# Order of work around stage changes in a fused attention and mixture-of-experts kernel

## The chip, the cores and the metric

The kernel runs on one core of one Trainium2 chip. The metric is the device time of one execution in microseconds (us); the median of three runs before the change is 936.39 us (933.29 to 939.31).

The engines of the core are TensorE (PE, matmuls; PEld, its weight loads), VectorE (DVE), ScalarE (ACT), GpSimd (POOL) and SyncE (SP). Each runs its own list of instructions in order. SP issues nearly all transfers here. SBUF is the memory of the engines, PSUM that of matmul results.

## The reference

Three parts follow each other; N is 1792 tokens of 768 numbers.

```
attn   = sigmoid(q @ k^T / 8 - log(448));  x = attn @ v          # 4 batches, 12 heads, 448 x 64
logits = x @ w_gate; each token is assigned to one of 8 experts, 224 tokens to each, greedily by logit
x[e]   = relu(x[e] @ w1[e]) @ w2[e]                              # 768 -> 1024 -> 768, every expert
h      = relu(x @ w_in); g = s * h * h + b                       # 768 -> 2048
out    = g @ w_out                                               # 2048 -> 768
```

All of it is float32. The kernel gets near that precision by splitting each operand into a high and a low half of a shorter format and summing three products: high·high, high·low, low·high.

## The kernel before, in words

**Stages.** Attention and routing come first and are not touched. Then come two passes, `Q` = 0 and 1, of two groups each (group `g` = 2Q + h). A group takes two experts (224 tokens each; 8 units of `w1`, 6 units of `w2`), then the *middle layer* on their 448 tokens: 16 units `f` of `w_in`, 18 matmuls of 448 columns each. After two groups comes the *output stage* of the pass: seven products (index `j`) of four units each, on 3 blocks of 128 tokens (Q = 0) or 4 (Q = 1), 6 matmuls of 384 columns per unit and block. The seven products are a Strassen-like scheme of a 2 x 2 block multiplication; sums of weight blocks for it (T1 to T4) are made on the chip.

**A unit of weights.** SP loads it into `raw` (4 buffers), ACT writes the high half `wh` (L204), DVE or POOL the low half `wl` (L215). `advance()` keeps these ahead of use: loads by 8 units, low halves by 4, high halves by 5.

**What stands around the stage changes.**

- `x_split(e, n)`: four calls transpose the gathered rows of expert `e` on PE (L667) and split them (ACT L669, DVE L670). For the first expert of the next group the calls come in the middle layer; for the second, in the first expert's units 1 to 4. The tiles are named `x` and have two buffers.
- The *late work* (`late_step`, L761 to L785) runs in the two middle layers of Q = 0 only. It turns the last eight blocks of `w_out`, which come as 64-bit numbers, into float32 (`to_float`, three steps; L152, L153, then L155, then L157) and makes the sums (L776 and L780 to L782), for four indices `u`: two per middle layer, one step per unit. Loads go into `orow`, sums into another buffer of the name `x`; the results are stored to DRAM, from where the output stage loads them as weights.
- `a_high` (ACT L827) and `a_low` (DVE L833) split the middle layer's result `gt` for the output stage, `a_sum` (DVE L818 to L822) adds parts of it. The first two pieces are split at the end of the middle layer, into `u`; the rest in the output stage, into the buffers `as`.
- The *results* of a product: after its fourth unit each block is copied (ACT L889) or added (DVE L892) from PSUM to the rows `orow`. Product 2 starts on the PSUM banks of product 1, product 6 on those of product 5.

The order on each engine is that of the program text; no planner stands behind it.

Of the kernel before, what the change touches and what calls it, by code (L numbers as in the profile page):

```python
# [30 lines left out]
KG = F2 // 128  # L31
HT = (128, CAP - 128)
DH = DM // 2
# [30 lines left out]
def tile_kernel(ctx, tc, qT, kT, v, wg, w1, w2, wi, wo, s2, b2, cst, out):  # L64
    nc = tc.nc
    V, A, G, T = nc.vector, nc.scalar, nc.gpsimd, nc.tensor
# [634 lines left out]
    def advance():  # L701
        while nu["dma"] < min(nu["use"] + 8, len(units)):
            w_dma()
        while nu["low"] < min(nu["use"] + 4, nu["high"]):
            w_low()
        while nu["high"] < min(nu["use"] + 5, len(units)):
            w_high()

    def expert(e, y):
        x = xg.pop(e)  # L710
        u = ml.tile([128, KF, 2, CAP], F32R, name="u")
        for f in range(KF):
            wh, wl = w_get()
            if f < KF - 2:
                half_mm(wh, wl, x, KD, AF.Relu, (u[:, f, 0], u[:, f, 1]), f < KF - 3)
                if f == KF - 3:
                    advance()
            else:
                short_mm(wh, wl, x, KD, (u[:, f, 0], u[:, f, 1]))
                if f == KF - 2:  # L720
                    advance()
            if 1 <= f <= 4:
                if e % 2 == 0:
                    x_split(e + 1, f - 1)
                if out_rows:
                    scatter(*out_rows.pop(0))
        sl = slice((e % 2) * CAP, (e % 2 + 1) * CAP)
        for d in range(KD):
            wh, wl = w_get()
            half_mm(wh, wl, u, KF, AF.Copy, (y[:, d, 0, sl], y[:, d, 1, sl]), d < KD - 1)  # L730
            if not e and d == 1:
                row_ids()

    def scatter(ids, row):
        G.memset(spacer, 0.0)
# [16 lines left out]
    def flat(t):  # L752
        return t.rearrange("p k c -> p (k c)")

    def late_step(u, k):
        o, x = late["o"], late["x"]
# [3 lines left out]
        s, c, d = (x[:, 768 * n:768 * n + 768] for n in range(3))  # L760
        first, second = LB + u, LB + 4 + u  # L761
        if k in (0, 4):
            to_float(a if k == 0 else b, r, raw, 0)
        elif k in (1, 5):
            to_float(a if k == 1 else b, r, raw, 1)
            nxt = second if k == 1 else first + 1
            if nxt < LB + 4 or k == 1:
                late_in(nxt)
        elif k == 2:
            to_float(a, r, raw, 2)  # L770
        elif k == 3:
            nc.sync.dma_start(c, flat(blocks[0][0][u]))
            nc.sync.dma_start(d, flat(blocks[1][0][u]))
        elif k == 6:
            to_float(b, r, raw, 2)
            V.tensor_sub(s, fa, fb)  # L776
            nc.sync.dma_start(flat(narrow[second]), fb)
            nc.sync.dma_start(flat(T3[u]), s)
        elif k == 7:
            V.tensor_sub(fa, fa, c)  # L780
            V.tensor_sub(c, c, s)
            V.tensor_sub(d, d, c)  # L782
            nc.sync.dma_start(flat(T1[u]), fa)
            nc.sync.dma_start(flat(T2[u]), c)
            nc.sync.dma_start(flat(T4[u]), d)  # L785

    stores, out_rows, late, pool = [], [], {}, {}
    na = {"sum": 0, "high": 0, "low": 0}
# [44 lines left out]
        V.tensor_sub(a[:, 1], part(st, i, operand[i // 4]), a[:, 0].bitcast(F32))  # L833
        na["low"] += 1

    def a_advance(st, n):
        while na["low"] < min(n + 3, na["high"]):
            a_low(st)
        while na["sum"] < min(n + 5, 28):
            a_sum(st)  # L840
        while na["high"] < min(n + 4, 28):
            a_high(st)

    def outputs(st):
# [19 lines left out]
        a_advance(st, 0)  # L864
        for j in range(7):
            spans = [[u] for u in range(4)] if j < 6 or not Q else [[0], [1], [2, 3]]
            for span in spans:
                ws = {u: [w.rearrange("p k c -> p (k c)") for w in w_get()] for u in span}
                for p in range(P):
                    acc = bank[j][p][:, :DH]  # L870
                    for u, c in ((u, c) for u in span for c in range(2)):
                        wh, wl = ws[u]
                        a = st["slots"][(4 * j + u) % st["ring"]]
                        cols = slice(c * DH, (c + 1) * DH)
                        hi, lo = (a[:, n, c, p * 128:(p + 1) * 128] for n in range(2))
                        T.matmul(acc, hi, wh[:, cols], start=(opens[j] and u == 0 and c == 0), stop=False,  # L876
                                 skip_group_check=True)
                        T.matmul(acc, hi, wl[:, cols], start=False, stop=False, skip_group_check=True)  # L878
                        T.matmul(acc, lo, wh[:, cols], start=False, stop=(u == 3 and c == 1), skip_group_check=True)  # L879
                advance()  # L880
                a_advance(st, 4 * j + span[-1] + 1)
                if span[-1] < 3:
                    continue
                for p in range(P):
                    acc = bank[j][p][:, :DH]
                    c11, c12 = (row[2 * p][:, d * DH:(d + 1) * DH] for d in range(2))
                    c21, c22 = (row[2 * p + 1][:, d * DH:(d + 1) * DH] for d in range(2))
                    if j in (0, 2, 3, 6):
                        A.copy({0: c11, 2: c22, 3: c21, 6: c12}[j], acc)  # L889
                    else:  # L890
                        dst = {1: c11, 4: c21, 5: c22}[j]
                        V.tensor_add(dst, acc, dst)  # L892
                    if j in (5, 6):
                        h = 6 - j
                        out_rows.append((tok[p][h], row[2 * p + h]))
                        if Q:
                            scatter(*out_rows.pop(0))

    for n in (0, 2, 1, 3):
        x_split(0, n)  # L900
# [5 lines left out]
    for Q in range(2):  # L906
        epool = ExitStack()
        pool["y"] = epool.enter_context(tc.tile_pool(name=f"yp{Q}", bufs=1))
        for h in range(2):
# [8 lines left out]
            for f in range(KG):  # L918
                wh, wl = w_get()
                p = ps_m.tile([128, 512], F32, name="acc")  # L920
                for k in range(KD):
                    full_mm(p[:, :S], wh[:, k], wl[:, k], y, k, k == 0, k == KD - 1)
                r = pool["y"].tile([128, S], F32, name="tmp", bufs=2)
                A.activation(r, p[:, :S], AF.Relu)  # L924
                V.scalar_tensor_tensor(r, r, sb2[:, 0:1], r, op0=ALU.mult, op1=ALU.mult)  # L925
                if h and f < KG // 2:
                    V.scalar_tensor_tensor(gn[:, f, 1], r, sb2[:, 1:2], gn[:, f, 0], op0=ALU.add, op1=ALU.subtract)
                else:
                    A.activation(gn[:, f, h], r, AF.Identity, bias=sb2[:, 1:2])
# [12 lines left out]
            gather(2 * g + 3)  # L942
        epool.close()
# [66 lines left out]
```

## Time and profile before

| | |
|---|---|
| median of 3 runs | 936.39 us |
| profiled execution | 934.25 us, of which the traced span is 932.4 us |
| PE busy | 890.1 us, 95% of the span |
| DVE busy | 625.1 us, 67% |
| ACT busy | 516.8 us, 55% |
| POOL busy | 137.3 us, 15% |
| data moved | 177.80 MB, mean 191 GB/s |

In the span, the first group begins at about 204 us, its middle layer at 272.8, the second group at 332 and its middle layer at 399.8. The first output stage starts at 459.9 us, the third group at 558, the fourth at 681, and the second output stage runs from 803.8 us to the end.

"Busy" is an average over all of that; where an engine stood idle, and what ended it, is in the list of waits. A time given in a trace row is the start, in us from the beginning of the span; the number behind it is the duration.

### The profile page before, as it was taken

Reading aid. Unit: us, or ns where it says so; the run is one execution under the profiler, and the core shown is the slowest. Engines: PE = TensorE matmul, PEld = TensorE weight load, DVE = VectorE, ACT = ScalarE, POOL = GpSimd, SP = SyncE. Lnnn points to the kernel's source line nnn. Section 1 sums busy time; section 2 is a strip of 40 time slices with the busy share of each in tenths; the row PEclk is TensorE's granted clock in tenths of the full one; section 3 lists DMA queues with packets and bytes.
Section 4 is the critical chain, followed back from the end, with each engine's and each line's share of the span. In section 5 each row is a group of like instructions: output and inputs, shape, how many; then the busy total and the mean of one; then the engine's idle time right before and its main releaser. Section 6 shows DMA issues by size and latency. Waiting matters only on the chain.

```text
span 932.4 us, 14229 instructions
## 1 busy us (share of the span) xinstructions
PE 890.1 (95%) x5291; PEld 769.1 (82%) x5291; DVE 625.1 (67%) x1005; ACT 516.8 (55%) x871; POOL 137.3 (15%) x131
## 2 busy tenths in 40 slices
PE   9999999789999979999799999999999999899997
PEld 4555545569889979999699999999989999899997
DVE  3777886638566787869767857864467764547680
ACT  6667667726555556643645546655565634554540
POOL 1000003213510034200000015410034100000003
PEclk9999999769999999999999999999999999999999
DMA  9989893855656776648643347753365633332313
GB/s 296 323 295 349 298 328 138 247 154 186 199 170 223 259 278 211 226 156 282 220 148 119 120 136 238 273 161 120 102 193 181 218 116 104 102 100 87 100 34 135
DMA packets 70184, 177.80 MB, mean 191 GB/s; under 512 B 8160, under 2 KB 25056, under 8 KB 70112
## 3 DMA queue, kind: packets, MB, share of 16 engines
q1 hardware_dynamic: 67840, 165.85, 54.4%
q0 software_dynamic: 2272, 11.01, 3.3%
q8 instruction: 42, 0.69, 0.3%
q14 instruction: 30, 0.25, 0.1%
HBM read 148.52 MB, written 28.31 MB: 190 GB/s over the span
## 4 chain that ended last, share of the span: by engine, by line
PE 56%; issue 23%; DVE 8%; DMA 5%; ACT 4%; POOL 3%; POOLq 0%; SPq 0%; ACTq 0%; DVEq 0%
PE pv L274 8%; PE psc L263 7%; PE acc L743 6%; PE acc L745 6%; PE acc L744 6%; PE acc L675 6%; DMA raw<-in_w_dram 4%; PE acc L879 3%; PE acc L876 3%; DVE wl L215 3%; PE acc L878 3%; PE acc L676 3%; ACT wh L204 2%; DVE y L689 1%; POOL wl L215 1%
## 5 line engine op out<-in xcount | busy, mean ns | idle before, releaser
L204 ACT CAST wh<-raw 128x768 fp32r<-128x768 f32 (+1 forms) x232 | 202.4, 879 | 115.7 <-issue 46.8
L215 DVE TENSOR_TENSOR wl<-raw,wh 128x768 fp32r<-128x768 f32 (+1 forms) x191 | 200.5, 1052 | 54.5 <-ACT wh L204 54.4
L215 POOL TENSOR_TENSOR wl<-raw,wh 128x768 fp32r<-128x768 f32 (+1 forms) x41 | 91.3, 2234 | 490.1 <-ACT wh L204 485.6
L743 PE MATMUL acc<-y,wh 128*128 128x448 f32 x384 | 141.2, 368 | 0.0
L744 PE MATMUL acc<-y,wh 128*128 128x448 f32 x384 | 140.4, 366 | 0.0
L745 PE MATMUL acc<-y,wl 128*128 128x448 f32 x384 | 140.3, 365 | 0.0
L675 PE MATMUL acc<-u,wh 128*128 128x448 f32 x384 | 121.7, 376 | 3.0 <-DVE u L699 2.9
L925 DVE SCALAR_TENSOR_TENSOR tmp<-tmp,sb 128x448 f32<-128x448 f32 x64 | 45.6, 712 | 83.5 <-ACT tmp L924 83.3
L676 PE MATMUL acc<-u,wl 128*128 128x224 f32 x384 | 101.4, 264 | 0.0
L675 PE MATMUL acc<-x,wh 128*128 128x448 f32 x288 | 95.0, 384 | 3.8 <-DVE x L670 3.4
L265 ACT ACTIVATE attn<-psc,nls 112x896 f32<-112x896 f32 x96 | 88.9, 1009 | 10.1 <-PE psc L263 10.1
L675 PEld LDWEIGHTS acc<-u,wh 128*128 128x128 f32 x384 | 72.1, 188 | 9.9 <-DVE u L699 4.6
L924 ACT ACTIVATE tmp<-acc 128x448 f32<-128x448 f32 x64 | 34.9, 546 | 80.1 <-PE acc L745 80.1
L274 PE MATMUL pv<-attn,vt 112*64 112x448 f32 x384 | 77.5, 545 | 0.0
L676 PE MATMUL acc<-x,wl 128*128 128x224 f32 x288 | 76.8, 267 | 0.5 <-DVE wl L215 0.5
L745 PEld LDWEIGHTS acc<-y,wl 128*128 128x128 f32 x384 | 72.1, 188 | 5.9
L743 PEld LDWEIGHTS acc<-y,wh 128*128 128x128 f32 x384 | 72.1, 188 | 5.8
L744 PEld LDWEIGHTS acc<-y,wh 128*128 128x128 f32 x384 | 72.2, 188 | 5.7
L676 PEld LDWEIGHTS acc<-u,wl 128*128 128x128 f32 x384 | 73.3, 191 | 0.0
L675 PEld LDWEIGHTS acc<-x,wh 128*128 128x128 f32 x288 | 54.9, 191 | 8.4 <-DVE x L670 3.9
L274 PEld LDWEIGHTS pv<-attn,vt 112*64 112x64 f32 x384 | 25.4, 136 | 42.9 <-issue 36.1
L680 DVE TENSOR_TENSOR tmp<-acc,tmp 128x224 f32<-128x224 f32 x96 | 36.9, 385 | 32.0 <-ACT tmp L679 32.0
(261 smaller groups left out, 1744.2 us busy)
## 6 DMA issues: line engine op xcount, KB each, us to landing
raw<-nw SPq DMA_DIRECT2D x88, 384.0 KB, 3.1
raw<-in_w_dram SPq DMA_DIRECT2D x64, 384.0 KB, 3.0
raw<-in_w_dram SPq DMA_DIRECT2D x48, 512.0 KB, 5.0
craw<-in_wi_dram SPq DMA_DIRECT2D x16, 768.0 KB, 4.5
raw<-mx SPq DMA_DIRECT2D x32, 384.0 KB, 2.8
nw<-co SPq DMA_DIRECT2D x24, 384.0 KB, 8.2
craw<-in_wo_dram SPq DMA_DIRECT2D x8, 768.0 KB, 4.2
orow<-in_wo_dram SPq DMA_DIRECT2D x8, 768.0 KB, 5.7
```

What stands on the lines that cost most here:

```text
L204: A.copy(h[:, :k], raws[i][:, :k])
L215: eng.tensor_sub(lo[:, :k], r[:, :k], h[:, :k].bitcast(F32))
L263: T.matmul(p[:, j, :S], kx[me, 1, c * CP:(c + 1) * CP], qx[me, 0], start=(m == 0), stop=(m == len(terms) - 1))
L265: A.activation(attn[n][:, :, c, :], p[:, :, :S], AF.Sigmoid, bias=nls[:CP], scale=1.0 / math.sqrt(D))
L274: T.matmul(pv[j * 64:(j + 1) * 64, :S], v[:, c, j * D:(j + 1) * D], a[:, j, c, :], start=(c == 0), stop=(c == NC - 1))
L675: T.matmul(p[:, :2 * CAP], wh[:, k], src[:, k].rearrange("p a s -> p (a s)"), start=(k == 0), stop=False)
L676: T.matmul(p[:, :CAP], wl[:, k], src[:, k, 0], start=False, stop=(k == n - 1))
L680: V.tensor_add(tt, p[:, :CAP], bs)
L743: T.matmul(p, wh, src[:, k, 0], start=first, stop=False)
L744: T.matmul(p, wh, src[:, k, 1], start=False, stop=False)
L745: T.matmul(p, wl, src[:, k, 0], start=False, stop=last)
L925: V.scalar_tensor_tensor(r, r, sb2[:, 0:1], r, op0=ALU.mult, op1=ALU.mult)
```

## The change

It moves work and adds or removes no computation.

- The next group's rows are split at units 3, 6, 9 and 12 of the middle layer, not 3, 7, 11 and 15.
- The late work follows a written plan: index `a` = 2h in units 0 to 4, `b` = 2h + 1 in units 4 to 12. The conversion for index 0 is begun in the second layer of expert 1 (`d` = 2, 3, 4), that for index 2 in units 13 and 14 of the first middle layer.
- The first two splits of `gt` are made at units 11 to 14 (`a_high` at 11 and 13, `a_low` at 12 and 14). Before, these were at 14 and 15, with the second `a_low` at the start of the output stage.
- At the end of a product the results are issued in turn with the low halves of weights, the low halves of `gt` and the sums; the high halves follow. Before, the results came behind all of these.

```diff
@@ -730,6 +739,8 @@
             if not e and d == 1:
                 row_ids()
+            if e == 1 and 2 <= d <= 4:
+                late_do(f"a{d - 2}", 0)
@@ -752,37 +763,46 @@
-    def late_step(u, k):
+    def late_do(what, u):
...
-        if k in (0, 4):
-            to_float(a if k == 0 else b, r, raw, 0)
-        elif k in (1, 5):
-            to_float(a if k == 1 else b, r, raw, 1)
...
+    def late_work(h, f):
+        a, b, c = 2 * h, 2 * h + 1, 2 * h + 2
+        plan = {0: [("a2", a) if h else None, ("b0", a), ("load", a)], 1: [("b1", a), ("b2", a)], 2: [("t3", a)],
+                3: [("t1", a), ("t2", a)], 4: [("t4", a), ("a0", b)], 5: [("a1", b), ("a2", b)], 7: [("load", b)],
+                8: [("b0", b)], 9: [("b1", b), ("b2", b)], 10: [("t3", b)], 11: [("t1", b), ("t2", b)],
+                12: [("t4", b)], 13: [None if h else ("a0", c)], 14: [None if h else ("a1", c)]}
...
-    def a_advance(st, n):
-        while na["low"] < min(n + 3, na["high"]):
-            a_low(st)
-        while na["sum"] < min(n + 5, 28):
-            a_sum(st)
+    def ahead(st, n, more=()):
...
+        w_dmas()
+        work, more = [w_lows, lows, sums], list(more)
+        while work or more:
+            for q in (work, more):
+                if q:
+                    q.pop(0)()
+        w_highs()
         while na["high"] < min(n + 4, 28):
             a_high(st)
@@ -877,24 +908,26 @@
-                advance()
-                a_advance(st, 4 * j + span[-1] + 1)
+                n = 4 * j + span[-1] + 1
                 if span[-1] < 3:
+                    ahead(st, n)
                     continue
...
+                ahead(st, n, [lambda p=p: result(p) for p in range(P)])
@@ -927,17 +960,17 @@
-                if f % 4 == 3:
-                    x_split(2 * g + 2, f // 4)
+                if f % 3 == 0 and 3 <= f <= 12:
+                    x_split(2 * g + 2, f // 3 - 1)
                 advance()
                 if not Q:
-                    late_step(2 * h + f // 8, f % 8)
-                if h and f == KG - 3:
+                    late_work(h, f)
+                if h and f == KG - 6:
                     st = start_out(Q)
                     st["ring"] = 6 - Q
-                if h and f >= KG - 2:
+                if h and f in (KG - 5, KG - 3):
                     a_high(st)
-                if h and f == KG - 1:
+                elif h and f in (KG - 4, KG - 2):
                     a_low(st)
```

In the plan `a0` to `a2` and `b0` to `b2` are the three conversion steps of the two blocks of an index; `load` fetches the two other blocks, `t3`, `t1`, `t2`, `t4` make and store the sums.

Three places in the order of the instructions follow. First VectorE at the change from the second middle layer (units 14 and 15) to the first output stage; L925 and L958 are the squares of a unit, L833 and L853 `a_low`, L776 to L782 and L785 to L794 the late sums. Before:

```order
L776 TENSOR_TENSOR x<-orow 128x768
L925 SCALAR_TENSOR_TENSOR tmp<-tmp,sb_76 128x448
L670 TENSOR_TENSOR x<-px,x 128x3x96
L215 TENSOR_TENSOR wl<-raw,wh 128x768
L780 TENSOR_TENSOR orow<-orow,x 128x768
L781 TENSOR_TENSOR x<-x 128x768
L782 TENSOR_TENSOR x<-x 128x768
L833 TENSOR_TENSOR u<-gt,u 128x768 x2
```

and in the changed kernel, from unit 12 on:

```order
L670 TENSOR_TENSOR x<-px,x 128x3x96
L215 TENSOR_TENSOR wl<-raw,wh 128x768
L794 TENSOR_TENSOR x<-x 128x768
L853 TENSOR_TENSOR u<-gt,u 128x768
L958 SCALAR_TENSOR_TENSOR tmp<-tmp,sb_76 128x448
L215 TENSOR_TENSOR wl<-raw,wh 128x768
L958 SCALAR_TENSOR_TENSOR tmp<-tmp,sb_76 128x448
L215 TENSOR_TENSOR wl<-raw,wh 128x768
L853 TENSOR_TENSOR u<-gt,u 128x768
L958 SCALAR_TENSOR_TENSOR tmp<-tmp,sb_76 128x448
L215 TENSOR_TENSOR wl<-raw,wh 128x768 x2
L853 TENSOR_TENSOR as_5376<-gt,as_5376 128x768
```

The row split, the late sums and both `a_low` now stand ahead of unit 15's square (the last L958 shown); behind it come weights, then the third `a_low`.

Second, VectorE at the change from the first group to the second, before (L680 is the first work of expert 2):

```order
L925 SCALAR_TENSOR_TENSOR tmp<-tmp,sb_76 128x448
L670 TENSOR_TENSOR x<-px,x 128x3x96
L215 TENSOR_TENSOR wl<-raw,wh 128x768
L780 TENSOR_TENSOR orow<-orow,x 128x768
L781 TENSOR_TENSOR x<-x 128x768
L782 TENSOR_TENSOR x<-x 128x768
L680 TENSOR_TENSOR tmp<-acc,tmp 128x224
```

and now, from unit 12 on:

```order
L670 TENSOR_TENSOR x<-px,x 128x3x96
L794 TENSOR_TENSOR x<-x 128x768
L958 SCALAR_TENSOR_TENSOR tmp<-tmp,sb_76 128x448
L215 TENSOR_TENSOR wl<-raw,wh 128x768
L152 TENSOR_SCALAR orow<-orow 128x768
L153 TENSOR_SCALAR orow<-orow 128x768
L958 SCALAR_TENSOR_TENSOR tmp<-tmp,sb_76 128x448
L155 SCALAR_TENSOR_TENSOR orow<-orow 128x768
L958 SCALAR_TENSOR_TENSOR tmp<-tmp,sb_76 128x448
L215 TENSOR_TENSOR wl<-raw,wh 128x768
L680 TENSOR_TENSOR tmp<-acc,tmp 128x224
```

Between unit 15's square and expert 2 there is now one low half of weights; the row split and the three sums have gone ahead.

Third, VectorE at the end of product 1 of the first output stage (L892 and L924 are results, L818 and L838 sums), before:

```order
L215 TENSOR_TENSOR wl<-raw,wh 128x768
L833 TENSOR_TENSOR as_5376<-gt,as_5376 128x768
L215 TENSOR_TENSOR wl<-raw,wh 128x768
L833 TENSOR_TENSOR as_5377<-gt,as_5377 128x768
L818 TENSOR_TENSOR gt<-gt 128x2x384
L892 TENSOR_TENSOR orow<-acc,orow 128x384 x3
L215 TENSOR_TENSOR wl<-raw,wh 128x768
```

and now:

```order
L853 TENSOR_TENSOR as_5377<-gt,as_5377 128x768
L215 TENSOR_TENSOR wl<-raw,wh 128x768
L924 TENSOR_TENSOR orow<-acc,orow 128x384
L853 TENSOR_TENSOR as_5378<-gt,as_5378 128x768
L924 TENSOR_TENSOR orow<-acc,orow 128x384
L838 TENSOR_TENSOR gt<-gt 128x2x384
L924 TENSOR_TENSOR orow<-acc,orow 128x384
L215 TENSOR_TENSOR wl<-raw,wh 128x768
```

The first result stands behind one low half of weights, where it stood behind that, a split and a sum.

## Rows read from the trace of the kernel before

**Rows 1.** The page, part 1: busy us (share of the span) xinstructions.
```profile
PE 890.1 (95%) x5291; PEld 769.1 (82%) x5291; DVE 625.1 (67%) x1005; ACT 516.8 (55%) x871; POOL 137.3 (15%) x131
```

**Rows 2.** Waits of PE: waiter <- who ended it: us in total, times, longest.
```profile
PE acc L879 <- DVE u L833: 9.5, 2, 6.9
...
PE px L667 <- DVE x L670: 3.9, 2, 3.1
PE acc L675 <- DVE x L670: 3.4, 2, 1.7
...
PE acc L876 <- DVE orow L892: 2.0, 3, 1.1
```

**Rows 3.** Timeline of PE, first output stage's start: start, duration, instruction [idle before].
```profile
467.30 0.69 PE L879 MATMUL acc<-wh,u 128*128 128x384 f32 x1 [6.85 <-DVE u L833]
...
470.35 0.41 PE L879 MATMUL acc<-wh,u 128*128 128x384 f32 x1
470.60 0.34 PE L876 MATMUL acc<-wh,u 128*128 128x384 f32 x1
```

**Rows 4.** Timeline of PE, second output stage's start.
```profile
808.41 0.51 PE L876 MATMUL acc<-wh,u 128*128 128x384 f32 x1
...
811.60 0.44 PE L878 MATMUL acc<-wl,u 128*128 128x384 f32 x1
```

**Rows 5.** Timeline of DVE, end of the second middle layer.
```profile
460.50 0.68 DVE L925 SCALAR_TENSOR_TENSOR tmp<-tmp,sb 128x448 f32<-128x448 f32 x1 [0.24 <-ACT tmp L924]
...
463.44 0.95 DVE L780 TENSOR_TENSOR orow<-orow,x 128x768 f32<-128x768 f32 x1
...
466.30 1.82 DVE L833 TENSOR_TENSOR u<-gt,u 128x768 fp32r<-128x768 f32 x2
```

**Rows 6.** Chain that ended last, change to the second group: start, us, what.
```profile
335.95 2.54 DVE orow L780
...
340.49 3.93 DMA mx<-x
...
345.08 0.57 DVE x L670
```

**Rows 7.** Timeline of DVE, end of product 1, first output stage.
```profile
488.31 0.96 DVE L215 TENSOR_TENSOR wl<-raw,wh 128x768 fp32r<-128x768 f32 x1 [1.29 <-ACT wh L204]
...
491.43 0.96 DVE L215 TENSOR_TENSOR wl<-raw,wh 128x768 fp32r<-128x768 f32 x1 [1.29 <-ACT wh L204]
...
493.17 0.95 DVE L818 TENSOR_TENSOR gt<-gt 128x768 f32<-128x768 f32 x1
494.04 1.48 DVE L892 TENSOR_TENSOR orow<-acc,orow 128x384 f32<-128x384 f32 x3
```

**Rows 8.** Timeline of PE, second layers of experts 5 and 7.
```profile
608.14 0.47 PE L675 MATMUL acc<-u,wh 128*128 128x448 f32 x1 [0.80 <-DVE u L699]
...
732.18 0.47 PE L675 MATMUL acc<-u,wh 128*128 128x448 f32 x1 [0.35 <-DVE u L699]
```

**Rows 9.** Groups of DVE instructions, 272 to 460 us: busy us, mean ns.
```profile
L155 DVE SCALAR_TENSOR_TENSOR orow<-orow 128x768 int32<-128x768 int32 x8 | 7.6, 952 | 0.0
...
L152 DVE TENSOR_SCALAR orow<-orow 128x768 int32<-128x768 int32 x8 | 4.4, 553 | 0.0
```

**Rows 10.** Timeline of DVE, last work of expert 1.
```profile
274.24 0.39 DVE L689 TENSOR_TENSOR y<-tmp,y 128x224 fp32r<-128x224 f32 x1 [0.45 <-ACT y L688]
```

**Rows 11.** Timeline of PE, first unit of the first middle layer.
```profile
275.81 0.36 PE L743 MATMUL acc<-y,wh 128*128 128x448 f32 x1
276.01 0.36 PE L744 MATMUL acc<-y,wh 128*128 128x448 f32 x1
```

**Rows 12.** Stretches: us, busy of PE, PEld, DVE, ACT, POOL, PEclk, DMA share, GB/s.
```profile
432.00:446.00 14.00, 14.00 (x71) 12.72 (x70) 11.86 (x17) 6.28 (x10) 0.00 (x0) 1.00 0.89 319
...
396.00:460.00 64.00, 64.00 (x327) 58.81 (x326) 49.25 (x70) 28.76 (x50) 1.28 (x1) 1.00 0.62 211
```

**Rows 13.** Timeline of ACT, first output stage's start.
```profile
463.54 1.56 ACT L827 CAST as<-gt 128x768 fp32r<-128x768 f32 x2
```

More of the change, by code (lines that the diff above doesn't have):

```diff
@@ L699, in short_mm, with w_dmas, w_lows, w_highs @@
         V.scalar_tensor_tensor(lo, p, 0.0, hi.bitcast(F32), op0=ALU.max, op1=ALU.subtract)
-    def advance():
+    def w_dmas():
         while nu["dma"] < min(nu["use"] + 8, len(units)):
             w_dma()
+    def w_lows():
         while nu["low"] < min(nu["use"] + 4, nu["high"]):
             w_low()
+    def w_highs():
         while nu["high"] < min(nu["use"] + 5, len(units)):
             w_high()
+    def advance():
+        w_dmas()
+        w_lows()
+        w_highs()
     def expert(e, y):
@@ L753, in flat @@
         return t.rearrange("p k c -> p (k c)")
-    def late_step(u, k):
-        o, x = late["o"], late["x"]
+    def late_do(what, u):
+        o = late["o"]
         a, b, r = (o[:, 768 * n:768 * n + 768] for n in (3 + u % 2, 5, 2))
@@ L759, in late_step @@
         fa, fb = a.bitcast(F32), b.bitcast(F32)
-        s, c, d = (x[:, 768 * n:768 * n + 768] for n in range(3))
-        first, second = LB + u, LB + 4 + u
-        if k in (0, 4):
-            to_float(a if k == 0 else b, r, raw, 0)
-        elif k in (1, 5):
-            to_float(a if k == 1 else b, r, raw, 1)
-            nxt = second if k == 1 else first + 1
-            if nxt < LB + 4 or k == 1:
-                late_in(nxt)
-        elif k == 2:
-            to_float(a, r, raw, 2)
-        elif k == 3:
+        if what[0] in "ab" and what[1:].isdigit():
+            step = int(what[1:])
+            to_float(a if what[0] == "a" else b, r, raw, step)
+            nxt = LB + 4 + u if what[0] == "a" else LB + u + 1
+            if step == 1 and (what[0] == "a" or u < 3):
+                late_in(nxt)
+            if what == "b2":
+                nc.sync.dma_start(flat(narrow[LB + 4 + u]), fb)
+            return
@@ L772, in late_step @@
+        s, c, d = (late["x"][:, 768 * n:768 * n + 768] for n in range(3))
+        if what == "load":
             nc.sync.dma_start(c, flat(blocks[0][0][u]))
             nc.sync.dma_start(d, flat(blocks[1][0][u]))
-        elif k == 6:
-            to_float(b, r, raw, 2)
+        elif what == "t3":
             V.tensor_sub(s, fa, fb)
-            nc.sync.dma_start(flat(narrow[second]), fb)
             nc.sync.dma_start(flat(T3[u]), s)
-        elif k == 7:
+        elif what == "t1":
             V.tensor_sub(fa, fa, c)
+            nc.sync.dma_start(flat(T1[u]), fa)
+        elif what == "t2":
@@ L781, in late_step @@
             V.tensor_sub(c, c, s)
+            nc.sync.dma_start(flat(T2[u]), c)
+        else:
             V.tensor_sub(d, d, c)
-            nc.sync.dma_start(flat(T1[u]), fa)
-            nc.sync.dma_start(flat(T2[u]), c)
             nc.sync.dma_start(flat(T4[u]), d)
+    def late_work(h, f):
[4 more added lines that the diff above has]
+                12: [("t4", b)], 13: [None if h else ("a0", c)], 14: [None if h else ("a1", c)]}
+        for job in plan.get(f, []):
+            if job:
+                late_do(*job)
@@ L834, in a_low, with lows, sums @@
         na["low"] += 1
-    def a_advance(st, n):
-        while na["low"] < min(n + 3, na["high"]):
-            a_low(st)
-        while na["sum"] < min(n + 5, 28):
-            a_sum(st)
+    def ahead(st, n, more=()):
+        def lows():
+            while na["low"] < min(n + 3, na["high"]):
+                a_low(st)
+        def sums():
+            while na["sum"] < min(n + 5, 28):
+                a_sum(st)
+        w_dmas()
+        work, more = [w_lows, lows, sums], list(more)
[3 more added lines that the diff above has]
+                    q.pop(0)()
+        w_highs()
         while na["high"] < min(n + 4, 28):
@@ L863, in outputs @@
             tok.append([idt[:, t - 1, 2 * Q + h:2 * Q + h + 1] if t else idl[:, h:h + 1] for h in range(2)])
-        a_advance(st, 0)
+        ahead(st, 0)
         for j in range(7):
@@ L879, in outputs, with result @@
                         T.matmul(acc, lo, wh[:, cols], start=False, stop=(u == 3 and c == 1), skip_group_check=True)
-                advance()
-                a_advance(st, 4 * j + span[-1] + 1)
+                n = 4 * j + span[-1] + 1
                 if span[-1] < 3:
+                    ahead(st, n)
                     continue
-                for p in range(P):
+                part_of = {0: (0, 0), 1: (0, 0), 2: (1, 1), 3: (1, 0), 4: (1, 0), 5: (1, 1), 6: (0, 1)}[j]
+                def result(p):
+                    t, d = part_of
+                    dst = row[2 * p + t][:, d * DH:(d + 1) * DH]
                     acc = bank[j][p][:, :DH]
-                    c11, c12 = (row[2 * p][:, d * DH:(d + 1) * DH] for d in range(2))
-                    c21, c22 = (row[2 * p + 1][:, d * DH:(d + 1) * DH] for d in range(2))
                     if j in (0, 2, 3, 6):
-                        A.copy({0: c11, 2: c22, 3: c21, 6: c12}[j], acc)
+                        A.copy(dst, acc)
                     else:
-                        dst = {1: c11, 4: c21, 5: c22}[j]
                         V.tensor_add(dst, acc, dst)
                     if j in (5, 6):
-                        h = 6 - j
-                        out_rows.append((tok[p][h], row[2 * p + h]))
+                        out_rows.append((tok[p][t], row[2 * p + t]))
                         if Q:
                             scatter(*out_rows.pop(0))
+                ahead(st, n, [lambda p=p: result(p) for p in range(P)])
     for n in (0, 2, 1, 3):
```

## The prediction

> **What bounds the kernel now.** I read the page's part 1 first: TensorE is busy for 890.1 of 932.4 us [rows 1], so it sets the time, and only what makes it wait, or slows it, can be won. Next its list of waits [rows 2]. The reader is to see four rows that belong to stage changes: 9.5 us for the low half of a piece of `gt` (L833), in two waits, the longest 6.9; 3.9 for the low half of expert rows inside an expert (3.1 of them one wait); 3.4 in two waits of 1.7 for the same thing at an expert's start; 2.0 in three waits for a result to leave its bank. Then the timeline of TensorE at both output stages' starts [rows 3, 4]: behind each long wait there is a stretch of slow steps. Then VectorE at the same places, for what stood ahead of the thing waited for [rows 5, 7], and the chain of waits at the second group [rows 6].
>
> **The change, part by part.** All sums stand against the profiled execution, 934.25 us, of which 932.4 is the span.
>
> *First splits of `gt`.* At the first output stage TensorE stands 6.85 us until L833 [rows 3]. On VectorE this split comes after unit 15's square (460.50), a row split, a low half and the three late sums (from 463.44), and starts at 466.30 [rows 5]. In the new order it is made in unit 12. Its input was finished in the middle layer before (index 0 of `gt`), so nothing holds it there. The wait goes: 6.85, and at the second output stage the other one of the row, 9.5 - 6.85 = 2.65 [rows 2, 3].
>
> *The clock behind these waits.* From 467.30 to 470.35 nine steps take 3.05 us [rows 3]; at full speed a unit of 18 such matmuls takes 3.12, the distance of two low halves of weights in this stage [rows 7], so 0.173 a step, and nine take 1.56. By its steps (0.34 each) TensorE ran near the lower of its two clock levels, 1.2 of 2.4 GHz, after standing still; that cost 1.49. From 808.41 to 811.60 ten steps take 3.19 against 1.73: 1.46 [rows 4]. Without the waits I take both as gone, 2.95; at worst both stay.
>
> What is late next there: the splits of pieces 2 and 3, made in the output stage as before. ScalarE makes their high halves at 463.54, 0.78 each [rows 13], VectorE the low ones after one low half of weights, so the first is ready near 463.54 + 0.78 + 0.96 + 0.91 = 466.2 (0.91 is half of the 1.82 in [rows 5]). TensorE, unheld, reaches unit 2 two units of 3.12 after the stage's start at about 460, at 466.2, and the low half is that unit's third matmul, 0.35 later. ScalarE has a row split and one high half fewer ahead of these than before, so there is more room than that. I take 0; the other end is a wait that takes the place of part of the old one (a rival).
>
> *Row splits at 3, 6, 9, 12.* The two waits of 1.7 [rows 2] are for the last quarter of the rows, split behind unit 15. It moves to unit 12, three units earlier. A unit is 18 steps of 0.20 [rows 11], 3.6 us, so it is 11 us earlier: 3.4 go. The same instructions lie elsewhere in the middle layer, where VectorE is busy 49.25 of 64 us in the fuller of the first two [rows 12]. Cost 0.
>
> *Late sums done by unit 12.* The wait of 3.1 in expert 2 is for a buffer `x` that still holds the last sum: the sums run from 335.95 (the first takes 2.54 us), the last store is issued at 340.49 and takes 3.93 to land, and only then are the rows of expert 3 split [rows 6]. Now this store is issued three units earlier, before expert 2 begins. The 3.1 go.
>
> *Results between splits.* At the end of product 1 the three results start at 494.04, behind low half, split and sum (491.43 to 494.04), and TensorE waits for the bank of the first one [rows 7]. Now the first result is next behind the low half of 491.43, so at about 492.3, 1.7 us sooner; the wait was 1.1 [rows 2]. The other two follow one split or sum apart (0.9 us), and TensorE needs their banks one block (3.12 / 3 = 1.04 us) apart, so they keep up. The three waits go: 2.0.
>
> *What it costs.* (1) Three conversion steps lie in the second layer of expert 1: at most 2 x 0.55 + 2 x 0.95 = 3.0 us of VectorE [rows 9]. Its last work for the layer now ends at 274.63 [rows 10]; TensorE reads that block's low half at 276.01 [rows 11]. Room 1.4. VectorE also idles ahead of it (0.45 in that row alone), so between 0 and 3.0 - 1.4 = 1.6 is lost; I take 0. (2) In the second middle layer units 0 to 5 are over-full: two elementwise steps of about 0.7 each (one is the 0.68 in [rows 5]), a low half of 0.96 and up to 2.0 of late work is 4.4 at most, against 3.6. VectorE falls back by up to 0.8 a unit, some 3 us, until the empty units 6 and 7. Cover: low halves run four units ahead, 14 us. If that cover were gone, TensorE would wait 3 us once. I take 0. (3) SyncE issues the late loads and stores between weight loads, in one queue. The dense units move, each five, two loads and four to five stores of 384 KB, one load of 768 KB and five weight loads of 384 KB: 5.5 MB in 18.2 us, 302 GB/s. The old order's dense stretch ran at 319 with TensorE busy 14.00 of 14.00 us [rows 12]. Cost 0; the other end is the slower rival.
>
> *What is given back.* An expert pair that starts without a wait finds VectorE and the loads less far ahead. The third group is such a start now, and waits 0.80 in its second half; the fourth, which began with a wait, only 0.35 [rows 8]; the second shows no such row. I let both end at 0.80: 0.45 + 0.80 = 1.25, and count 1.6 for what smaller waits may join. Bounds: 0 and twice that.
>
> **Sum:** 6.85 + 2.65 + 2.95 + 3.4 + 3.1 + 2.0 = 20.95, less 1.6: 19.35. 934.25 - 19.35 = 914.9. The profiled execution lies 2.1 under the median of the runs (936.39); I add a little of that and say **915.5**, its own range 911.5 to 919.
>
> A rule of the Trainium skill speaks against one piece. TensorE: Matmul & The Clock Gate, Architectural detail, says that ScalarE and VectorE take their work strictly first in, first out. The trace agrees: the results at 494.04 wait behind a sum they have nothing to do with [rows 7]. By that rule each result now holds what stands behind it, which is the first rival.
>
> **The rivals.**
>
> *Held splits, 919.* A result waits for its block of the last unit, and high halves, low halves and sums stand behind it in order. On ScalarE the next high half starts one result later, 1.48 / 3 = 0.49 [rows 7], at eight product ends; if it were on the path, 8 x 0.49 = 3.9 would come back: 934.25 - 19.35 + 3.9 = 918.8. For it: ScalarE's high half does gate VectorE's low half (1.29 idle, [rows 7]). Against it: that low half is for a unit three to four ahead, some 9 us. Chance 0.09.
>
> *The entry still waits, 923.* Pieces 2 and 3 or the first weights come late, and half of the entry waits stays, with the slow clock in full: 0.5 x 9.5 + 2.95 = 7.7, giving 922.6. For it: my margin above was small. Against it: it counts ScalarE work that no longer stands ahead. Chance 0.09.
>
> *The waits are not what they seem, 932.* Another thing, ready only just before, stood behind each (weights, a transfer), and takes over; only the results' 2.0 goes: 932. Against it: VectorE's own list shows it at work on late sums up to the split. Chance 0.04.
>
> *Slower: the late transfers crowd the weight loads, 946.* Place: units 0 to 4 and 8 to 12 of both first-pass middle layers. If the transfers kept only the mean of that stretch, 211 GB/s [rows 12], 5.5 MB would take 26.1 us and not 18.2, 7.9 over, four times 31: 934.25 - 19.35 + 31 = 946. It decides once the excess passes 19.35 / 4 = 4.8 us each, a rate below 5.5 MB / 23.0 us = 239 GB/s, and only with the four units of lead used up. Against it: 319 GB/s was held without a wait. Chance 0.03.
>
> **How the numbers follow.** Forecast 0.75, rivals 0.09, 0.09, 0.04 and 0.03. The range: below, no give-back (913.3) and runs that lie up to 3.1 under their median (933.29), so 910.5; above, the second rival and a little, 924. Outside lie the last two rivals and about a tenth of the others. One per cent, 9.4 us, is about what a measurement of this kernel can tell from no change. Faster by over that: forecast and the first two rivals, 0.92 with a little taken off; within: the third and mishaps, 0.05; slower: the last, 0.03.
>
> **What would show it.** TensorE's list of waits without L833 and without results; waits for expert rows only in the first group. The steps at both output stages' starts at 0.17 throughout. VectorE's `a_low` for pieces 0 and 1 before unit 15's square. The last late store landed before expert 2 begins. Expert 1's second layer with no wait for `y`. I am wrong if a wait for weights or `as` stands at an output stage's start, if TensorE waits for weight loads in the first pass's middle layers, or if waits in the second layers of experts 3 and 7 grow past 2 us.

## The result and the profile after

| | before | changed | ratio, 95% interval |
|---|---|---|---|
| first comparison, median (4 and 4 runs) | 935.86 us | 911.8 us (910.12 to 913.04) | 0.9739 [0.9704, 0.9775] |
| second comparison (11 and 6 runs) | 934.88 us | 913.69 us (911.86 to 917.93) | 0.9783 [0.9755, 0.9811] |
| profiled execution (span) | 934.25 us (932.4) | 913.04 us (911.2) | |

The kernel is 21 to 24 us faster. The forecast was 915.5, its range 910.5 to 924. The second comparison is the run `again` below. One execution each of `no_late` and `hold_two` took about 3047 us; the medians given for these two contain it, their ratios do not.

The page of the changed kernel, busy times and the granted clock in 40 slices:

```profile
PE 886.7 (97%) x5291; PEld 767.1 (84%) x5291; DVE 622.8 (68%) x1005; ACT 517.0 (57%) x871; POOL 134.0 (15%) x131
...
PEclk9999999869999999999999999999999999999999
```

The busy times are those of [rows 1] within 4 us; the span is 21 shorter. What went is mostly idle time. TensorE's waits in the changed kernel, the first seven groups (total us, times, longest; lines below L600 belong to attention and routing, PEq is TensorE's sequencer):

```profile
PE pa L464 <- DVE aw L462: 5.7, 9, 0.7
PE acc L675 <- DVE u L699: 3.1, 4, 0.9
PE pb L501 <- ACT junk L489: 2.3, 4, 1.1
PE acc L667 <- DMA xr<-xs,idx: 1.9, 1, 1.9
PE px L667 <- DVE x L670: 1.2, 2, 0.8
PE psc L350 <- DVE zero L346: 1.2, 1, 1.2
PE acc L667 <- PEq L621: 0.6, 1, 0.6
```

Against [rows 2], the split of `gt`, the results and the wait at an expert's start are gone; of the waits for expert rows inside an expert 1.2 of 3.9 are left, 0.78 of these in the first group and 0.43 in the fourth, where the text had expected none. At the first output stage TensorE goes on from the middle layer without a gap (start, duration; L907, L909 and L910 were L876, L878 and L879):

```profile
456.24 0.37 PE L756 MATMUL acc<-y,wl 128*128 128x448 f32 x1
456.44 0.34 PE L907 MATMUL acc<-wh,u 128*128 128x384 f32 x1
456.62 0.33 PE L909 MATMUL acc<-wl,u 128*128 128x384 f32 x1
456.79 0.34 PE L910 MATMUL acc<-wh,u 128*128 128x384 f32 x1
```

The steps are 0.17 to 0.18, where [rows 3] has 0.34 for the nine behind the wait. VectorE there:

```profile
449.01 0.95 DVE L794 TENSOR_TENSOR x<-x 128x768 f32<-128x768 f32 x1
449.87 0.95 DVE L853 TENSOR_TENSOR u<-gt,u 128x768 fp32r<-128x768 f32 x1
...
455.53 0.95 DVE L853 TENSOR_TENSOR u<-gt,u 128x768 fp32r<-128x768 f32 x1
457.29 0.69 DVE L958 SCALAR_TENSOR_TENSOR tmp<-tmp,sb 128x448 f32<-128x448 f32 x1 [0.81 <-ACT tmp L957]
...
460.31 1.82 DVE L853 TENSOR_TENSOR as<-gt,as 128x768 fp32r<-128x768 f32 x2
```

The last late sum (449.01) and both first splits are done before unit 15's square (457.29); in [rows 5] they came behind it. The last late store of the first middle layer is issued at 327.1 and the stores there take at most 5.0 to land; expert 2 begins at 333.2. Piece 2 is split by 460.31 + 0.91 = 461.2. TensorE needs it at the third matmul of unit 2, 456.44 + 2 x 3.12 + 0.35 = 463.0: 1.8 us of room.

The end of product 1 on VectorE (L924 is the result, L892 before):

```profile
479.38 0.96 DVE L215 TENSOR_TENSOR wl<-raw,wh 128x768 fp32r<-128x768 f32 x1 [1.29 <-ACT wh L204]
480.25 0.55 DVE L924 TENSOR_TENSOR orow<-acc,orow 128x384 f32<-128x384 f32 x1
480.72 0.95 DVE L853 TENSOR_TENSOR as<-gt,as 128x768 fp32r<-128x768 f32 x1
481.59 0.55 DVE L924 TENSOR_TENSOR orow<-acc,orow 128x384 f32<-128x384 f32 x1
482.06 0.95 DVE L838 TENSOR_TENSOR gt<-gt 128x768 f32<-128x768 f32 x1
482.92 0.55 DVE L924 TENSOR_TENSOR orow<-acc,orow 128x384 f32<-128x384 f32 x1
```

The first result starts 0.87 behind the low half, where [rows 7] has 2.61; none of the three waits on TensorE, and TensorE waits on none.

Time by stage, from one stage's first matmul to the next one's, in the two profiled executions:

| stage | before | changed | difference |
|---|---|---|---|
| experts, group 1 | 68.28 | 68.95 | +0.66 |
| experts, group 2 | 67.53 | 63.25 | -4.28 |
| output stage 1 | 97.88 | 87.53 | -10.35 |
| experts, group 3 | 63.34 | 63.07 | -0.27 |
| experts, group 4 | 64.53 | 62.85 | -1.68 |
| output stage 2 | 128.60 | 122.91 | -5.69 |
| four middle layers together | 237.75 | 237.98 | +0.23 |

Four stages hold the gain, 22.0 us. They are the four that the forecast named. In `again` the second group takes 64.38, so its gain is 3.2 to 4.3; a wait of 1.05 for gathered rows stands there.

### The profile page after: what moved, and what is told of

Its sections match the earlier page's. It is cut to its first block, busy times and chain, and to the rows that moved or that the text cites. A ratio compares the mean times of both kernels' runs of the same rounds, so it can differ in the third digit from the quotient of the medians.

```text
span 911.2 us, 14237 instructions
## 1 busy us (share of the span) xinstructions
PE 886.7 (97%) x5291; PEld 767.1 (84%) x5291; DVE 622.8 (68%) x1005; ACT 517.0 (57%) x871; POOL 134.0 (15%) x131
## 4 chain that ended last, share of the span: by engine, by line
PE 63%; issue 23%; DMA 5%; DVE 4%; ACT 3%; POOL 3%; POOLq 0%; ACTq 0%; DVEq 0%; SPq 0%
PE acc L675 8%; PE pv L274 8%; PE psc L263 7%; PE acc L754 6%; PE acc L755 6%; PE acc L756 6%; DMA raw<-in_w_dram 4%; PE acc L676 4%; PE acc L907 3%; PE acc L910 3%; PE acc L909 3%; DVE wl L215 2%; ACT wh L204 1%; POOL wl L215 1%; PE px L439 1%
## 5 line engine op out<-in xcount | busy, mean ns | idle before, releaser
L215 DVE TENSOR_TENSOR wl<-raw,wh 128x768 fp32r<-128x768 f32 (+1 forms) x191 | 203.6, 1068 | 47.3 <-ACT wh L204 47.0
L215 POOL TENSOR_TENSOR wl<-raw,wh 128x768 fp32r<-128x768 f32 (+1 forms) x41 | 88.3, 2160 | 490.9 <-ACT wh L204 488.5
L958 DVE SCALAR_TENSOR_TENSOR tmp<-tmp,sb 128x448 f32<-128x448 f32 x64 | 44.7, 698 | 73.8 <-ACT tmp L957 73.8
L680 DVE TENSOR_TENSOR tmp<-acc,tmp 128x224 f32<-128x224 f32 x96 | 36.8, 384 | 31.3 <-ACT tmp L679 31.1
```

The costliest lines, as they stand in the source:

```text
L215: eng.tensor_sub(lo[:, :k], r[:, :k], h[:, :k].bitcast(F32))
L680: V.tensor_add(tt, p[:, :CAP], bs)
```

## The experiments

The theory: each wait goes with the part that makes its cause earlier, and where two things stood ahead of one wait, taking away one exposes the other. The rival: each part is worth the length of the wait it aims at, whatever the others do. Four runs do one part alone, three leave one out (none leaves out the results), one repeats the changed kernel, one triples a step suspected of a cost, two go on from the changed kernel.

**rows**: the kernel before, with

```diff
-                if f % 4 == 3:
-                    x_split(2 * g + 2, f // 4)
+                if f % 3 == 0 and 3 <= f <= 12:
+                    x_split(2 * g + 2, f // 3 - 1)
```

> The kernel before with the row splits at units 3, 6, 9 and 12 alone. Theory (waits share their causes): at the fourth group the 1.7 us go; at the second they only move, since the late store that holds the buffer x still lands at its old time, so the wait inside expert 2 grows from 3.1 to about 4.4. At the first output stage the low half of gt comes about 1.5 us earlier, as a row split no longer stands ahead of it. Total -3.6, ratio about 0.996. Rival (each wait is worth its own length, on its own): both 1.7 go, nothing else changes, -3.4, and the wait in expert 2 stays at 3.1. The totals do not tell the two apart; the length of the wait in expert 2 does.

Measured: 933.11 against 935.17, ratio 0.998 [0.996, 0.9999]. TensorE's waits (start, duration, [idle before]):

```profile
338.86 0.52 PE L667 MATMUL px<-ident,xr 128*128 128x128 f32 x3 [1.04 <-DMA xr<-xs,idx]
...
346.63 0.47 PE L667 MATMUL px<-ident,xr 96*128 96x96 f32 x3 [3.17 <-DVE x L670]
```

The wait at expert 2's start went, but 4.2 us (1.04 for the gathered rows, 3.17 for the buffer) now stand inside expert 2 where 3.1 did, and the group gained nothing (68.72 against 67.53, with a stretch of slow clock behind the second wait). The wait for the buffer alone did not grow to the 4.4 of the theory; only the two waits together come near it, and why the gathered rows were waited for was not tried. So the 1.7 is not won in the second group, against the rival, but the theory's step to that is only half shown. The first output stage's wait fell to 5.53 (6.85 - 1.5 = 5.35 expected). The fourth group gained 1.78.

**late**: the kernel before, with the plan of late work (`late_do`, `late_work`, and the three calls in expert 1) alone.

```diff
-                    late_step(2 * h + f // 8, f % 8)
+                    late_work(h, f)
```

> The kernel before with the late work on the new plan alone. Theory: the wait of 3.1 in expert 2 goes, the 1.7 at its start stays; at the first output stage the three late sums (2.9 us) no longer stand ahead of the low half of gt, so 6.85 becomes about 4. Total -6, ratio about 0.9935. Rival: only the 3.1 goes, -3.1, ratio 0.9967, because the output stage waits for its own first split whatever stands ahead. If the conversions in expert 1 cost what they could at worst, 1.6 us come back as a wait for y at the start of the first middle layer.

Measured: 930.25, ratio 0.9949 [0.9928, 0.9971]. The first output stage's start:

```profile
461.48 0.69 PE L890 MATMUL acc<-wh,u 128*128 128x384 f32 x1 [4.00 <-DVE u L844]
```

6.85 became 4.00, as expected from the three sums alone; the wait inside expert 2 went. Theory (0.9935) and rival (0.9967) both lie in the interval; the 4.00 tells them apart. The wait at expert 2's start did not stay at 1.7 but grew to 2.44 (and is 2.44 again in no_rows). In the trace the square of unit 14 is longer than before; here it is before, then in `late`:

```profile
329.27 0.97 DVE L925 SCALAR_TENSOR_TENSOR tmp<-tmp,sb 128x448 f32<-128x448 f32 x1 [1.23 <-ACT tmp L924]
```

```profile
328.90 2.09 DVE L936 SCALAR_TENSOR_TENSOR tmp<-tmp,sb 128x448 f32<-128x448 f32 x1
```

The second ran beside a GpSimd low half (328.56, 1.95), and the row split stands behind it; no run took this apart. No wait for `y`.

**splits**: the kernel before, with the first two splits early.

```diff
-                if h and f == KG - 3:
+                if h and f == KG - 6:
...
-                if h and f >= KG - 2:
+                if h and f in (KG - 5, KG - 3):
                     a_high(st)
-                if h and f == KG - 1:
+                elif h and f in (KG - 4, KG - 2):
                     a_low(st)
```

> The kernel before with the first two splits of gt at units 11 to 14 alone. Theory: both waits at the output stages' starts go (6.85 and 2.65) with the slow clock behind them (2.95), but in the first one the late sums still run until 466.3 and then a low half of weights stands ahead of the split of piece 2, so TensorE waits there for 1 to 2 us. Total -10.5 to -11.5, ratio about 0.988. Rival: all 12.45 go, ratio 0.9867, and no wait for the buffers as.

Measured: 923.38, ratio 0.9887 [0.9855, 0.992]. Both entry waits are gone and a new one stands two units on, at piece 2, behind the late sums:

```profile
466.62 0.44 PE L879 MATMUL acc<-wh,as 128*128 128x384 f32 x1 [2.02 <-DVE as L833]
```

The rival had no such wait; the ratios of both (0.988 and 0.9867) lie in the interval. This part alone is half of the gain, and it does need the late sums out of the way for the rest.

**results**: the kernel before, with `ahead` and the results between its steps.

```diff
-                advance()
-                a_advance(st, 4 * j + span[-1] + 1)
+                n = 4 * j + span[-1] + 1
...
+                ahead(st, n, [lambda p=p: result(p) for p in range(P)])
```

> The kernel before with the results of a product issued between low halves and sums, and the high halves behind them, alone. Theory: the three waits for results go, -2.0, ratio 0.998; the long waits at the output stages' starts stay as they were. Rival (held splits): the high halves behind the results come late and cost up to 3.9, so the time is 0 to 2 us longer than before, ratio 1.000 to 1.002, with waits for wl or as in the units that follow a product's end.

Measured: 931.82, ratio 0.9969 [0.9952, 0.9986]. The three waits for results are gone, no other came in the output stages, and both entry waits are as they were (6.85 and 2.66):

```profile
PE acc L899 <- DVE u L842: 9.5, 2, 6.9
```

The held-splits rival is out: its ratio was 1.000 or more.

By the medians the four parts alone give 2.1, 4.9, 11.8 and 3.4 us, 22.1 in all, and the whole change gives 21 to 24. The totals therefore show no interplay of the parts; the waits and stage times do, in both directions: in the second group parts fall short alone, and at the first output stage `late` and `splits` each shorten the same 6.85.

**no_late**: the changed kernel, with the old `late_step` at its old units and without the three calls in expert 1.

```diff
-                    late_work(h, f)
+                    late_step(2 * h + f // 8, f % 8)
```

> The changed kernel with the late work back at its old times. Theory: with rows, first splits and results moved but the late store still at unit 15, expert 2 waits about 4.2 for its buffer x (as in the run with rows alone), and the first output stage waits 0.5 to 1.5 for piece 2. The time is 5 to 6 longer than the changed kernel's 911.8, so about 917, ratio 0.981. Rival (each part is worth its own wait): only 3.1 longer, 915, ratio 0.978.

Measured: 919.17, ratio 0.9818 [0.9778, 0.9859]. Against the changed kernel's stages the second group takes 4.55 more and the first output stage 1.59, of which 1.30 is the wait for piece 2:

```profile
467.27 0.44 PE L899 MATMUL acc<-wh,as 128*128 128x384 f32 x1 [1.30 <-DVE as L842]
```

6.1 together: the late work on time is worth 6 us here, where its own wait was 3.1. Part of the 4.55 is a slow stretch behind a wait of 2.74 in expert 2. By the ratios the intervals of no_late and of the second comparison overlap, and those of no_rows and of the second comparison as well; what these two runs show rests on their waits and stages.

**no_rows**: the changed kernel, with `f % 4 == 3` again.

```diff
-                if f % 3 == 0 and 3 <= f <= 12:
-                    x_split(2 * g + 2, f // 3 - 1)
+                if f % 4 == 3:
+                    x_split(2 * g + 2, f // 4)
```

> The changed kernel with the row splits back at units 3, 7, 11 and 15. Theory: the waits at the starts of experts 2 and 6 come back, 1.7 to 2.4 and 1.7, nothing else of size, since at the output stage only piece 2 stands behind the row split and it has room. 3.4 to 4.1 longer than 911.8, about 915.6, ratio 0.979. Rival: the row split of unit 15 also makes piece 2 late, a wait of about 1 for the buffers as on top, 917, ratio 0.980.

Measured: 917.21, ratio 0.9814 [0.9784, 0.9843]. The waits are 2.44 and 1.69, with slow clock behind the first; none for `as`:

```profile
333.55 0.47 PE L675 MATMUL acc<-x,wh 128*128 128x448 f32 x1 [2.44 <-DVE x L670]
```

The stages of the second and fourth groups: +4.35 and +1.32. By the medians the same edit gives 2.1 us alone and 3.5 to 5.4 with the others.

**no_splits**: the changed kernel, with `a_high` and `a_low` at their old units.

```diff
-                if h and f in (KG - 5, KG - 3):
+                if h and f >= KG - 2:
                     a_high(st)
-                elif h and f in (KG - 4, KG - 2):
+                if h and f == KG - 1:
                     a_low(st)
```

> The changed kernel with the first two splits of gt back at units 14 and 15 and the output stage's start. Theory: with late sums and row split already out of the way, the first output stage still waits for the square of unit 15 and one low half of weights, some 2.5, and the second 2.65 as before; the slow clock may follow either, 1.5 each. 5 to 8 longer than 911.8, about 918, ratio 0.982. Rival (the late sums were what made the split late): the first wait is below 0.5, only the second stays; 3 to 4 longer, 915.5, ratio 0.979.

Measured: 921.47, ratio 0.9845 [0.9811, 0.9878]. The waits are 2.61 and 2.66, and the clock fell behind each. The stretch behind the first and the one after it (us; busy PE, PEld, DVE, ACT, POOL; granted clock; DMA share, GB/s):

```profile
459.60:462.80 3.20, 3.17 (x10) 3.17 (x11) 2.77 (x4) 1.87 (x3) 0.00 (x0) 0.50 0.40 123
463.00:466.00 3.00, 3.00 (x19) 3.00 (x18) 1.55 (x3) 1.57 (x2) 0.00 (x0) 1.00 0.35 122
```

Ten matmuls in 3.2 us at a granted 0.50 (1.2 GHz), 19 in 3.0 us at 1.00; at 0.173 a step the ten would have taken 1.73, so the slow clock cost 1.5. The two output stages lost 4.40 and 4.61, each a wait of 2.6 to 2.7, some 1.5 of slow clock and 0.3 to 0.5 besides. The rival's wait below 0.5 did not come: with late sums and row split out of the way the first split is still late by itself.

**again** and **double**: the changed kernel once more, and the changed kernel with the first conversion step in expert 1 done three times.

```diff
-                late_do(f"a{d - 2}", 0)
+                for _ in range(3 if d == 2 else 1):
+                    late_do(f"a{d - 2}", 0)
```

> The changed kernel once more, to stand beside the three that follow on the same chip: 911 to 913, ratio 0.974 to 0.976. The waits left in the middle of the experts (3 in all, for the low halves of the last two hidden units) and the slow clock behind them in expert 1 may differ between executions.

> The changed kernel with the first conversion step of index 0 in expert 1 done three times instead of once: 2.2 us more of VectorE work there (4 x 0.55), the output unchanged. Theory (there is room of 1.4 us before TensorE reads the last block of y, and 0.5 of idle time): the work is mostly hidden, a wait for y of 0.3 to 0.8 appears at the start of the first middle layer, under 0.1% in time, ratio to before within 0.001 of the changed kernel's. Rival (the conversions there were already on the path, and are what was lost): the whole 2.2 shows, ratio 0.0024 above the changed kernel's.

Measured: again 913.69, ratio 0.9783 [0.9755, 0.9811], a little over the expected 911 to 913; double 914.24, 0.9781 [0.9757, 0.9805]. The rival's 0.0024 is no more than these intervals; the trace tells. `double` has one wait for `y`:

```profile
273.79 0.47 PE L755 MATMUL acc<-y,wh 128*128 128x448 f32 x1 [0.38 <-ACT y L688]
```

2.2 us of added work show as an idle time of 0.38. The conversions as written, with no such wait in the changed kernel or in `again`, are hidden.

**hold_one** and **hold_two** go on: what is left to wait for in [rows 8] is the low half of the last two hidden units (L699), behind a low half of weights. hold_one issues the weight work of unit 6 after unit 7's result; hold_two that of units 5 and 6. The edit of hold_one:

```diff
                 short_mm(wh, wl, x, KD, (u[:, f, 0], u[:, f, 1]))
-                if f == KF - 2:
+                if f == KF - 1:
                     advance()
```

> The changed kernel with the weight work that follows hidden unit 6 of each expert issued behind unit 7's result. Theory (waits in the middle of the experts arise because a low half of weights, 1.2 us, stands ahead of the last hidden unit's low half): the wait for the last unit goes in each expert, 2 to 2.5 us of the 3.1 in all, and with it perhaps the slow clock in expert 1 (1.5). 2 to 3.5 shorter than the changed kernel, ratio lower by 0.002 to 0.004. Rival (VectorE is short of time there in any order): the wait moves to weights in the second layer, same time.

> The changed kernel with the weight work that follows hidden units 5 and 6 issued behind unit 7's result, two rounds of it. Theory: both waits of a pair go, all 3.1, with the slow clock in expert 1: 3 to 4.5 shorter than the changed kernel, ratio lower by 0.003 to 0.005, if the weights for the second layer's units 1 and 2 come in time. Rival: these weights are now late (three high halves of 1.05 and three low halves of 1.2 fall in the first unit of the second layer, 2.5 us), new waits for wl there of 1 us or more per expert, 8 us longer in all.

Measured: hold_one 907.34, ratio 0.9709 [0.9683, 0.9735]; hold_two 908.61, 0.9722 [0.9695, 0.9749]. hold_one is 6.3 us under the changed kernel by the medians, on the same chip, and beats both kernels. No wait for `u` is left in its list, and none in the second layers. VectorE there in hold_one:

```profile
251.78 1.22 DVE L215 TENSOR_TENSOR wl<-raw,wh 128x1024 fp32r<-128x1024 f32 x1
252.91 0.68 DVE L699 SCALAR_TENSOR_TENSOR u<-acc,u 128x224 fp32r<-128x224 f32 x2
253.51 1.21 DVE L215 TENSOR_TENSOR wl<-raw,wh 128x1024 fp32r<-128x1024 f32 x1
```

Both hidden units' low halves now run back to back. The gain is about twice what was expected. hold_two is 5.1 us under the changed kernel and cannot be told from hold_one; its rival, 8 us longer, is out (two waits for low halves of weights, 0.46 and 0.32). In hold_one the first group takes 63.08 against 68.20 in `again`, 5.1 of it; 1.6 of that are two waits (0.71 and 0.91) and about 1.4 the slow clock behind them (13 matmuls in 3.40 us, 2.03 at full speed by 0.157 each, half of the 0.314 that a pair of 448 and 224 columns takes behind it), shown by

```profile
258.00:261.40 3.40, 3.40 (x13) 3.13 (x13) 1.52 (x2) 2.40 (x4) 1.43 (x1) 0.50 0.65 209
```

in `again`. What the rest of that group's difference is (it has waits for loads that vary between executions) stays open. In the eleven profiles without this edit the first group takes 65.7 to 69.3, in hold_one and hold_two 63.08 and 64.08; the profiled execution of hold_one is its fastest, 3.4 under its median.

## Why the prediction was right

*First splits.* Right in mechanism and nearly in size: both entry waits went, and doing without this part brings back 2.6 at each. Pieces 2 and 3 were what was late next, as the text said, though with 1.8 us of room where its times left 0.35; `splits` and `no_late` show the wait (2.02 and 1.30) once the late sums stand ahead.

*The clock.* Right here: no slow stretch at either output stage. That a wait of this length costs the clock was taken from two rows, and it is not certain. Of 14 waits of 2.0 to 3.2 us behind the first group, in the profiles of before and of the seven runs from rows to no_splits, eight were followed by a fall of the clock to 0.50 within 5 us of their start, and six were not.

*Row splits and late sums.* Nearly right in sum (1.7 + 3.1 = 4.8 forecast, 4.28 measured in the second group, with a new wait of 0.50 in expert 3; 1.7 and 1.68 in the fourth). The text listed them as two separate gains of 3.4 and 3.1. The runs show that in the second group neither comes in full without the other: with `rows` the waits inside expert 2 grew by 1.1, with `late` the one at its start grew by 0.75, and the group gained nothing in `rows` and 1.64 in `late`.

*Results.* Right: 2.0 forecast, three waits gone, in the changed kernel and alone; the first result of product 1 comes 1.74 sooner behind its low half, where the text had 1.7. No run left this part out.

*Sizes.* The two output stages gave 16.0, the terms for them sum to 14.5 (6.85 + 2.65 + 2.95 + 2.0). The "idle before" of a row begins where the matmul before it is modelled to end, 0.34 after its start, but the next could have started 0.17 after. This row of the kernel before

```profile
460.11 0.34 PE L878 MATMUL acc<-wl,u 128*128 128x384 f32 x1
```

and the 467.30 of [rows 3] are 7.19 apart; less a normal step of 0.17 that is 7.02, not 6.85. Five waits in these stages (two at the entries, three for results) would make 0.85 of the 1.5 by this; the rest was not traced.

*The give-back* of 1.6 was wrong in where it lay. In the place that the text named, experts 3 and 7 wait 0.50 and 0.09, where 0.80 was put for each. The largest loss of the changed kernel is in the first group, 0.66, where two waits of 0.86 were followed by slow clock:

```profile
259.00:262.30 3.30, 3.10 (x11) 2.88 (x12) 1.67 (x3) 2.08 (x3) 0.71 (x1) 0.50 0.75 248
```

The kernel before has waits of 0.69 and 0.86 there and kept its clock in the profiled execution; in `double`, waits of 0.70 and 0.86 kept it too, while `rows` and `splits`, which have the old conversions, lost it. So the fall does not go with the conversions moved there; what decides it is not shown.

*The costs taken as 0* were 0: no wait for `y`, none for weight loads in the first pass's middle layers, so the slower rival did not happen. Late units of its dense stretch, in the changed kernel's second middle layer, moved 233 GB/s, less than the 302 that the text worked out and than the 319 of [rows 12]; all five units, 426.4 to 445.2, moved 247:

```profile
432.00:446.00 14.00, 14.00 (x74) 12.89 (x73) 11.10 (x15) 8.56 (x14) 0.09 (x1) 1.00 0.69 233
```

Against the profiled execution the forecast was 914.9, and 913.04 was measured. The output stages gave 1.6 more than their terms. Given back were 0.5 in the second and fourth groups and 0.8 in places that the text did not name, 1.3 in all against 1.6: that the sum came near is luck. The 915.5 lies 1.8 to 3.7 above the two medians, 0.6 of it added for the median of before.

## What to carry to other kernels

Before pricing a moved step, write down everything that stands ahead of the waiting instruction on its engine and the next thing that will be late; price edits that act on one wait together, since alone each can be worth less, or both can claim the same time. Work whose input is long finished should be issued before the last units of a stage, not at the change, and what TensorE will read next goes ahead of what it reads several units later (hold_one: one moved call, 6 us by the medians). Take the cost of a TensorE wait from start to start less a normal step, and add a chance of slow clock behind it.

## What the runs showed of the hardware

The clock fell to 0.50 behind waits far shorter than the 6.85 of the kernel before, down to a pair of 0.70 and 0.86 us, 1.4 apart, in `splits`, and not each time: such a pair at 256 us kept full clock in `double` (0.70 and 0.86) and lost it in `again` (0.71 and 0.91). Where it was worked out, a fall cost 1.4 to 1.5 us (1.49 and 1.46 in the kernel before, 1.5 in no_splits, 1.4 in `again`).

A VectorE step of 0.95 us took 2.5 when it ran beside a GpSimd one: the first late sum in [rows 6] before (335.95, 2.54), and another one after (321.61; the row ahead of it is a sum at its usual length). The GpSimd steps at their side, before and after, come last:

```profile
320.63 0.95 DVE L788 TENSOR_TENSOR orow<-orow,x 128x768 f32<-128x768 f32 x1
321.61 2.49 DVE L791 TENSOR_TENSOR x<-x 128x768 f32<-128x768 f32 x1
```

```profile
335.40 2.25 POOL L215 TENSOR_TENSOR wl<-raw,wh 128x768 fp32r<-128x768 f32 x1 [1.72 <-ACT wh L204]
```

```profile
321.35 1.94 POOL L215 TENSOR_TENSOR wl<-raw,wh 128x768 fp32r<-128x768 f32 x1 [56.97 <-ACT wh L204]
```

Both VectorE steps end 0.8 us behind the GpSimd one: 338.49 against 337.65, and 324.10 against 323.29.

The Trainium skill, SBUF — State Buffer, Terms, has VectorE and GpSimd share a port pair that one of them holds for a whole instruction; these rows agree with that, and no run here took it apart.
